# A fused spectral filter and MLP on one core: the sync queue in program order in the dense part as well

## The chip, the core and the metric

One NeuronCore of a Trainium2 chip. Its engines have queues of their own: PE (TensorE, matrix products into PSUM, with PEld loading the weights), ACT (ScalarE), DVE (VectorE), POOL (GpSimd) and SP (SyncE), which computes nothing here and issues DMAs. ACT and POOL issue some DMAs too. Each queue takes its instructions strictly in turn, so an instruction that waits on a semaphore holds up all behind it. The metric is the device time of one run in microseconds; lower is better.

## The reference, cut to what matters

```python
# x (8, 3008, 256) f32; filt_r, filt_i (1505, 256) f32
X = np.fft.rfft(x, axis=1)
Y = X * (filt_r + 1j * filt_i)[None]
x2 = np.fft.irfft(Y, n=3008, axis=1).astype(np.float32).reshape(24064, 256)
h = x2 @ w_in                       # w_in (256, 2048), float64
out = ((h - np.tanh(h)) @ w_out).astype(np.float32)   # w_out (2048, 256)
```

## The kernel before, in words

**Transforms.** 3008 is 64 x 47, so a transform is done as small matrix products in stages. `first` multiplies x by a 64-point matrix and writes `ct1` in DRAM; `middle` reads it back turned (tile `a2`, load_a2, L329), multiplies by a 47-point matrix (`pz`, L377), by the filter (`ft`, L335; the tiles `uv`, `zs`) and by the inverse matrix (`pe`, L358), and writes `ct2`; `last` reads that as `e2` (L409, L412), does the last product (`pu`) and leaves tokens in `ut` and combinations of them in `tu`. Matrices of middle come in as `fg` (load_slots, L322). The batches are taken as five units, `UNITS = [(0,), (1, 2), (3, 4), (5, 6), (7,)]`.

**Dense part.** The tokens form 48 groups of up to 512 (6 for a single batch, 12 for a pair). A group has four dense steps U (u = 0 to 3), each with 512 of the 2048 hidden columns: `up` (seven products of half-size blocks in place of eight), `shrink` for the step before (the activation, on ACT, DVE and POOL) and `down` for the one before that (accumulated in four PSUM banks over the four steps). Each dense step is cut into five quarters, at whose ends `t(k)`, k = 0 to 4, runs what is put between: a step of `first` or `middle` of the next unit, by the due times in `steps`, a stage of `late` (conversion of the last three eighths of the raw float64 weights, two raw tiles at a time) at even k, a stage of `copies` at odd k. A group is 20 quarters long. While unit 0's 24 dense steps run, first and middle of unit 1 are done among them, and so on.

**Stores.** When a group's accumulation is done, `down` leaves tile `o` in `stores`. At k = 2 of the next dense step `store` transposes it on DVE into `ot` (L624, one buffer) and issues 32 DMAs of 16 KB (12 KB in a unit's short last chunk) on the sync queue (L634).

**Copies.** `filters_d` zeroes some rows and then copies the filters from their input layout to `filt` in DRAM, for the units 1 to 4, one chunk of four frequencies in each of eight stages; `filters_of(c, filt_d)` issues at least six DMAs from DRAM to DRAM on the sync queue (L793). Unit 0 uses its own filters instead: `filters_of(c)` with no target loads a chunk into SBUF through POOL's queue (also L793), with a memset on POOL for the first three chunks, and `double_filters` copies it to the other half of the partitions on ACT (L818).

**Prologue.** Before the dense part, first (`first0`) and middle of unit 0 and the conversion of the first five eighths of the weights (raw loads, L195) run under `tc.manual_schedule()`: all queues in program order. Its last load is e2 of group 0. Then `last(0)` and the first two raw loads of `late` are traced with no order given.

**What sets the order.** The dense loop ran under `tc.manual_schedule(engines=order)` with PE, ACT, DVE and POOL: these take program order. SP is not among them; for it the framework's scheduler places each DMA by its own model as soon as its operands and buffers allow, so a DMA traced in the dense loop whose input is there from the start can stand among those of the prologue. Buffers are handed out by tag: a load into a tile waits until the tile that had the buffer has been read for the last time (`x` has three buffers, `a2`, `ft`, `fg`, `e2` two).

Of the kernel before, what the change touches and what calls it, by code (L numbers as in the profile page):

```python
# [140 lines left out]
def kernel(  # L141
# [9 lines left out]
    nc = tc.nc  # L151
    V, G, ACT = nc.vector, nc.gpsimd, nc.scalar
# [13 lines left out]
    def dram(t, off, dims):  # L166
        return bass.AP(tensor=t, offset=off, ap=[list(d) for d in dims])
# [100 lines left out]
    def halves(p, r, n):  # L268

        return [(h, slice(64 * h, 64 * h + 64), r + HALF * h, min(n, NR - r - HALF * h))  # L270
                for h in range(2) if r + HALF * h < NR]
# [144 lines left out]
    def widths(p, c):  # L416

        r, n = CHUNKS[p][c]
        return [128 if len(UNITS[p]) == 2 or r + j + HALF < NR else 64 for j in range(n)]
# [132 lines left out]
        gs[U] = (blocks, t, w)  # L552
        yield

    accs, stores = {}, []

    def down(U):

# [56 lines left out]
    def store(i, o):  # L615


        p, c = groups[i]
        r, n = CHUNKS[p][c]
        ws_ = widths(p, c)  # L620
        total = sum(ws_)
        ot = dn.tile([128, 2, CH * 128], F32, tag="ot", bufs=1, name="ot")
        for h in range(2):
            V.transpose(ot[:, h, 0:total], o[:, h, 0:total])  # L624
        b = UNITS[p][0]
        if len(UNITS[p]) == 2:
            blocks = [(r + 32 * q * NR, n, 32 * q) for q in range(4)]
        else:
            blocks = [(r_h + 32 * q * NR, n_h, rows.start + 32 * q)
                      for _, rows, r_h, n_h in halves(p, r, n) for q in range(2)]  # L630
        for h in range(2):
            for k in range(4):
                for row, m, lo in blocks:
                    nc.sync.dma_start(  # L634
                        dram(out.tensor, (b * SEQ + row) * DM + h * 128 + 32 * k,
                             [[NR * DM, 32], [DM, m], [1, 32]]),
                        ot[32 * k:32 * k + 32, h, :].rearrange(
                            "p (j c) -> p j c", c=128)[:, 0:m, lo:lo + 32])

    def bounded(z):  # L640

# [96 lines left out]
    with tc.tile_pool(name="tr", bufs=2) as tr:  # L738
        with tc.tile_pool(name="pro", bufs=1) as pro, \
# [83 lines left out]
            def turned(g3, t):  # L823


                ACT.copy(t[0:RP], g3[IM:IM + RP])
                ACT.mul(t[IM:IM + RP], g3[0:RP], -1.0)
# [11 lines left out]
            with tc.manual_schedule():  # L839
                nc.sync.dma_start(wf1, wf1_d)  # L840
                V.memset(near_b, B)
                V.memset(exp_b, -896.0)
                xs = [load_x0(0, (0, 4, 8))]
                ws = weights(tiles0, range(5), 3)
                xs += [load_x0(1), load_x0(2)]

                pad = pro.tile([64, DM], F32, name="pad")
                G.memset(pad, 0.0)
                G.dma_start(dram(ct1[0], NR * 64 * DM, [[DM, 64], [1, DM]]), pad)
                fts = {0: filters_of(0), 1: filters_of(1)}  # L850
                gx = [pro.tile([IM + RP, 4, RP2], F32, name=f"gx{k}") for k in range(2)]
                for t in gx:
                    G.memset(t[32:64], 0.0)
                next(ws)
                for c in range(3):
                    for k, _ in enumerate(first0(xs[c], c)):
                        if k == 3 or k == 1 and c > 0:
                            next(ws)
                G.dma_start(s2, s2_d)
                a2 = {0: load_a2(0, 0, False)}  # L860
                mats = {0: load_slots(0, pro), 1: load_slots(1, pro)}
                next(ws)
                double_filters(fts[0], 0)
                turned(mats[0][1], gx[0])
                waiting = []

                def back0():
                    j, uv, zs = waiting.pop(0)
                    c = j // 2
                    pe = z0("pe", [128, 2, DM])  # L870
                    for i in range(2):
                        k = (2 * j + i) % 4
                        nc.tensor.matmul(pe[0:RP2, i], mats[c][1][:, k], uv[0:IM + RP, i],
                                         start=True, stop=False)
                        nc.tensor.matmul(pe[0:RP2, i], gx[c % 2][:, k], zs[0:IM + RP, i],
                                         start=False, stop=True)
                    e1 = tr.tile([RP2, 2, DM], F32, tag="e1", bufs=2, name="e1")
                    ACT.copy(e1, pe[0:RP2])
                    ACT.dma_start(dram(ct2[0], 2 * j * RP2 * DM,
                                       [[DM, RP2], [2 * RP * DM, 2], [1, DM]]), e1)  # L880

                for j in range(NK // 2):
                    c = j // 2
                    if j % 2 == 0 and c + 1 < NK // 4:
                        a2[c + 1] = load_a2(0, c + 1, False)
                        if c + 2 < NK // 4:
                            mats[c + 2] = load_slots(c + 2, pro)
                            fts[c + 2] = filters_of(c + 2)
                    pz = z0("pz", [128, 2, DM])
                    for i in range(2):  # L890
                        k = (2 * j + i) % 4
                        nc.tensor.matmul(pz[:, i], mats[c][0][0:R2, k],
                                         a2[c][0:R2, k * DM:k * DM + DM], start=True, stop=True)
                    if waiting:
                        back0()
                    uv = tr.tile([128, 2, DM], F32, tag="uv", bufs=2, name="uv")
                    zs = tr.tile([128, 2, DM], F32, tag="zs", bufs=2, name="zs")
                    ft = fts[c][:, :, j % 2 * 2:j % 2 * 2 + 2]
                    V.tensor_mul(uv, pz, ft[:, 0])
                    V.tensor_mul(zs, pz, ft[:, 1])  # L900
                    waiting.append((j, uv, zs))
                    next(ws, None)
                    if j % 2 and c + 1 < NK // 4:
                        double_filters(fts[c + 1], c + 1)
                        turned(mats[c + 1][1], gx[(c + 1) % 2])
                    if j == NK // 2 - 2:
                        fs = first(1, z1)
                        next(fs)
                back0()
                for _ in ws:  # L910
                    pass
                e2s[0] = load_e2(*groups[0])


        with tc.tile_pool(name="dn", bufs=2) as dn, \
                tc.tile_pool(name="ps", bufs=1, space=bass.MemoryType.PSUM) as ps:

            psums.append(ps)
            for _ in last(0, z1):
                pass  # L920

            def tiles1(k, dtype, n):

# [21 lines left out]
                    yield  # L945

            late, copies = weights(tiles1, range(5, 8), 2), filters_d()
            next(late)
            total = 4 * len(groups)
            order = {nc.tensor.engine, ACT.engine, V.engine, G.engine}  # L950
            with tc.manual_schedule(engines=order):
                for U in range(total + 2):
                    i, u = divmod(U, 4)
                    if U < total:
                        p, c = groups[i]
                        if c == 0 and u == 0:
                            units = 4 * len(CHUNKS[p])
                            steps, done = [], 0
                            if p + 1 < len(UNITS):
# [3 lines left out]
                                lo, hi = 1.6 * units, 5 * units - 17  # L963
# [27 lines left out]
                    def t(k):  # L991


                        nonlocal ms, done
                        if k == 2 and stores:
                            store(*stores.pop())
                        if U >= total:
                            return
                        pos = 20 * c + 5 * u + k
                        if u == 3 and k in (0, 2) and i + 1 < len(groups):  # L1000
                            next(lasts)
                        elif done < len(steps) and steps[done] <= pos:
                            if done < n_f:
                                next(fs)
                            else:
                                next(ms)
                            done += 1
                            if done == n_f:
                                ms = middle(p + 1, z1)
                                next(ms)  # L1010
                        if i == len(groups) - 1 and k in (0, 2, 4):
                            next(bounds, None)
                        if k in (0, 2, 4):
                            next(late, None)
                        elif U > 0:
                            next(copies, None)
# [11 lines left out]
                            t(k)  # L1028
                for w in stores:
                    store(*w)  # L1030

    within = nc.values_load(count[0:1, 0:1], min_val=0, max_val=128)
    with tc.If(within < 128):
# [33 lines left out]
```

## Time and profile before

| | us |
|---|---|
| median of 7 runs | 2883.11 (2880.23 to 2887.02) |
| the profiled execution | 2884.76 |
| its span | 2883.0 |
| PE busy | 2749.3 |
| PE busy, from 300 to 2800 us | 2464.5 of 2500 |
| first dense product (`x`, L470) starts at | 130.2 |
| last store (32 DMAs) starts at | 2861.5 |

The page counts busy time by engine and cuts the span in 40 slices, one digit each, in tenths. Windows give the same for stretches that one names, with the share of time that the 16 DMA engines were busy. A row of waits reads "engine, line that waited <- what ended the wait: us in total, times, longest". SPq is SP's queue: a DMA's row there is the time SP took to issue it, not the transfer.

### The profile page before, as it was taken

The numbers are of one execution on the slowest core, as the hardware profiler recorded it, in microseconds if no ns is written. First come the engines' busy times: TensorE is split into PE (matmuls) and PEld (weight loads), VectorE is DVE, ScalarE is ACT, GpSimd is POOL, SyncE is SP. The second block draws the span as 40 slices with busy tenths as digits, with TensorE's granted clock in tenths as the row PEclk, the third lists the DMA queues.
The fourth block names the chain that finished last, engine by engine and source line by source line (L and its number), as shares of the span: only waits on it lengthen the run. The fifth ranks groups of instructions, "written<-read, shape, count | busy, mean of one in ns | idle before, by whom it ended". The sixth has DMA issues, their size and how long they took to land.

```text
span 2883.0 us, 36472 instructions
## 1 busy us (share of the span) xinstructions
PE 2749.3 (95%) x12474; PEld 2278.6 (79%) x12474; DVE 1983.3 (69%) x2214; ACT 1871.4 (65%) x2460; POOL 1747.7 (61%) x1379
## 2 busy tenths in 40 slices
PE   4789999999999999999999999999999999999996
PEld 2567677888878787888877887888888888888885
DVE  3585666766767777766676777766777777777765
ACT  3566666666667676666666776666666666666663
POOL 4345777445677767645576777655466666555544
PEclk7899999999999999999999999999999999999998
DMA  8763433232133222222222232312123222110100
GB/s 244 211 188 100 112 102 91 82 101 83 49 72 88 76 67 58 65 86 81 72 68 75 68 79 72 76 42 66 36 54 77 54 53 49 31 28 15 22 8 16
DMA packets 328030, 217.47 MB, mean 75 GB/s; under 512 B 229053, under 2 KB 280373, under 8 KB 327642
## 3 DMA queue, kind: packets, MB, share of 16 engines
q1 hardware_dynamic: 273464, 162.00, 22.9%
q10 hardware_dynamic: 52418, 49.82, 5.7%
q0 software_dynamic: 1952, 3.22, 0.5%
q8 instruction: 100, 1.64, 0.2%
q14 instruction: 96, 0.79, 0.1%
HBM read 138.81 MB, written 79.17 MB: 76 GB/s over the span
## 4 chain that ended last, share of the span: by engine, by line
PE 67%; ACT 10%; DVE 9%; POOL 4%; issue 4%; DMA 3%; SPq 1%; ACTq 1%; DVEq 0%; POOLq 0%
PE o L577 26%; PE x L470 17%; PE z L470 8%; PE y L470 5%; PE pe L358 3%; DVE h L531 3%; PE pu L434 3%; ACT y L526 2%; PE pz L377 2%; PE pf L298 2%; ACT y L527 2%; ACT u L476 1%; POOL t L452 1%; DVE h L535 1%; DVE uv L392 1%
## 5 line engine op out<-in xcount | busy, mean ns | idle before, releaser
L577 PE MATMUL o<-t,wd 128*128 128x256 f32 (+2 forms) x3072 | 779.0, 376 | 1.8 <-POOL t L451 1.3
L531 DVE TENSOR_TENSOR h<-h,y 128x1024 f32<-128x1024 f32 (+2 forms) x384 | 588.6, 1533 | 252.6 <-ACT y L527 252.5
L449 POOL TENSOR_TENSOR t<-h 128x512 f32<-128x512 f32 (+2 forms) x192 | 240.2, 1251 | 741.3 <-DVE h L535 561.2
L577 PEld LDWEIGHTS o<-t,wd 128*128 128x128 f32 x3072 | 582.1, 191 | 75.1 <-POOL t L451 1.9
L470 PE MATMUL x<-tu,wu 128*128 128x256 f32 (+2 forms) x2304 | 589.5, 378 | 14.0 <-ACT u L476 13.0
L577 PE MATMUL o<-h,wd 128*128 128x256 f32 (+2 forms) x2304 | 581.3, 375 | 0.2 <-DVE h L535 0.2
L535 DVE SCALAR_TENSOR_TENSOR h<-sq,h 128x1024 f32<-128x1024 f32 (+2 forms) x384 | 566.3, 1475 | 21.2 <-DVE h L531 0.9
L470 PEld LDWEIGHTS x<-tu,wu 128*128 128x128 f32 x2304 | 428.4, 190 | 156.5 <-issue 72.7
L577 PEld LDWEIGHTS o<-h,wd 128*128 128x128 f32 x2304 | 430.8, 190 | 71.1 <-issue 18.5
L532 ACT ACTIVATE sq<-y,near_b 128x1024 f32<-128x1024 f32 (+2 forms) x384 | 435.3, 1134 | 5.6 <-DVE h L535 0.9
L476 ACT COPY s<-x 128x512 f32<-128x512 f32 (+2 forms) x192 | 110.8, 577 | 461.7 <-PE x L470 450.7
L526 ACT ACTIVATE y<-h 128x1024 f32<-128x1024 f32 (+2 forms) x384 | 400.1, 1042 | 14.8 <-ACT e L361 7.2
L527 ACT ACTIVATE y<-y 128x1024 f32<-128x1024 f32 (+2 forms) x384 | 399.3, 1040 | 12.1
L452 POOL TENSOR_TENSOR t<-t,h 128x512 f32<-128x512 f32 (+2 forms) x192 | 308.7, 1608 | 0.0
L476 ACT COPY u<-x 128x512 f32<-128x512 f32 (+2 forms) x384 | 219.3, 571 | 80.4 <-PE x L470 33.1
L393 POOL TENSOR_TENSOR zs<-zs,ft 128x512 f32<-128x512 f32 x112 | 166.9, 1490 | 139.5 <-ACT zs L391 139.4
L450 POOL TENSOR_TENSOR t<-h,t 128x512 f32<-128x512 f32 (+2 forms) x192 | 241.5, 1258 | 15.1
L451 POOL TENSOR_TENSOR t<-h 128x512 f32<-128x512 f32 (+2 forms) x192 | 249.5, 1299 | 0.0
L394 POOL TENSOR_TENSOR uv<-uv,zs 128x512 f32<-128x512 f32 x112 | 211.7, 1890 | 16.0 <-DVE uv L392 7.8
L470 PE MATMUL x<-ut,wu 128*128 128x256 f32 (+2 forms) x768 | 200.4, 384 | 14.2 <-DVE h L506 13.0
L470 PE MATMUL z<-tu,wu 128*128 128x256 f32 (+2 forms) x768 | 193.9, 375 | 1.6 <-DVE h L512 1.6
L470 PE MATMUL z<-ut,wu 128*128 128x256 f32 (+2 forms) x768 | 195.0, 376 | 0.0
(112 smaller groups left out, 3237.5 us busy)
## 6 DMA issues: line engine op xcount, KB each, us to landing
a<-ct SPq DMA_DIRECT2D x64, 384.0 KB
ct<-e ACTq DMA_DIRECT2D x128, 192.0 KB
ft<-filt SPq DMA_DIRECT2D x96, 256.0 KB
out_dram<-ot SPq DMA_DIRECT2D x1408, 16.0 KB
ct<-a ACTq DMA_DIRECT2D x80, 256.0 KB
x_sb<-in_x_dram SPq DMA_DIRECT2D x69, 256.0 KB
e<-ct SPq DMA_DIRECT2D x33, 512.0 KB
fg<-fg SPq DMA_DIRECT2D x40, 392.0 KB
```

Of the source, the lines that this page charges most:

```text
L449: G.tensor_sub(t[0], b[0][1], b[0][0])
L450: G.tensor_sub(t[1], b[1][1], t[0])
L451: G.tensor_sub(t[2], b[1][1], b[0][1])
L452: G.tensor_sub(t[3], t[1], b[1][0])
L470: nc.tensor.matmul(bank[:, k], wu[:, q - 1, (2 * u + k) * 128:(2 * u + k + 1) * 128], rhs[q - 1], start=(first and k == 0), stop=True, ski ...
L476: ACT.copy(t, X)
L526: ACT.activation(y[k], ht[k], AF.Arctan, scale=S)
L527: ACT.activation(y[k], y[k], AF.Square)
L531: V.tensor_mul(ht[k], ht[k], y[k])
L532: ACT.activation(sq[k], y[k], AF.Square, bias=near_b, scale=A)
L535: V.scalar_tensor_tensor(out=ht[k], in0=sq[k], scalar=K, in1=ht[k], op0=ALU.add, op1=ALU.mult)
L577: nc.tensor.matmul(product(q), wd[:, q - 1, (2 * u + k) * 128: (2 * u + k + 1) * 128], rhs[q - 1][:, k], start=(u == 0 and k == 0 and q == ...
```

## The change

SP joins the engines in program order for the dense part, and `last(0)` and the first raw loads of `late` move inside that block. `store` no longer issues its 32 DMAs but appends them to a list; `store_some(4)`, called in every quarter right after it, issues four, so that a group's stores take eight quarters; what is left goes out at the end. In the prologue the second chunk of unit 0's filters, on POOL's queue, is loaded after the three rounds of `first0` and the load of `s2` instead of before them.

```diff
-    accs, stores = {}, []
+    accs, stores, outs = {}, [], []
...
         for h in range(2):
             for k in range(4):
                 for row, m, lo in blocks:
-                    nc.sync.dma_start(
+                    outs.append((
                         dram(out.tensor, (b * SEQ + row) * DM + h * 128 + 32 * k,
                              [[NR * DM, 32], [DM, m], [1, 32]]),
                         ot[32 * k:32 * k + 32, h, :].rearrange(
-                            "p (j c) -> p j c", c=128)[:, 0:m, lo:lo + 32])
+                            "p (j c) -> p j c", c=128)[:, 0:m, lo:lo + 32]))
+
+    def store_some(n):
+        for dst, src in outs[:n]:
+            nc.sync.dma_start(dst, src)
+        del outs[:n]
...
-                fts = {0: filters_of(0), 1: filters_of(1)}
+                fts = {0: filters_of(0)}
...
                 G.dma_start(s2, s2_d)
+                fts[1] = filters_of(1)
...
             psums.append(ps)
-            for _ in last(0, z1):
-                pass
...
             late, copies = weights(tiles1, range(5, 8), 2), filters_d()
-            next(late)
             total = 4 * len(groups)
-            order = {nc.tensor.engine, ACT.engine, V.engine, G.engine}
-            with tc.manual_schedule(engines=order):
+            with tc.manual_schedule():
+                for _ in last(0, z1):
+                    pass
+                next(late)
                 for U in range(total + 2):
...
                         if k == 2 and stores:
                             store(*stores.pop())
+                        store_some(4)
                         if U >= total:
                             return
...
                 for w in stores:
                     store(*w)
+                store_some(len(outs))
```

## The prediction

> **What bounds the kernel now.** I read the page first, for the engine that is busy and the slices in which it is not.
>
> ```profile
> span 2883.0 us, 36472 instructions
> PE 2749.3 (95%) x12474; PEld 2278.6 (79%) x12474; DVE 1983.3 (69%) x2214; ACT 1871.4 (65%) x2460; POOL 1747.7 (61%) x1379
> PE   4789999999999999999999999999999999999996
> DMA  8763433232133222222222232312123222110100
> ```
>
> PE is busy for 2749.3 of 2883.0 us, so all that an order of DMAs can win lies in 133.7 us of idle PE. The first slices (72 us each) hold most of it, and there DMA shows 8, 7, 6. The view by windows splits this up.
>
> ```profile
> core 0: us, PE busy (x) PEld busy (x) DVE busy (x) ACT busy (x) POOL busy (x), PEclk, DMA share, GB/s
> 20.00:40.00 20.00, 6.52 (x12) 2.14 (x10) 9.16 (x19) 6.70 (x13) 4.64 (x6) 0.66 0.96 304
> 40.00:60.00 20.00, 6.91 (x16) 5.06 (x17) 7.21 (x15) 5.51 (x8) 4.10 (x7) 0.50 0.81 223
> 60.00:80.00 20.00, 15.22 (x59) 10.27 (x58) 15.49 (x31) 14.46 (x21) 12.98 (x21) 0.93 0.93 254
> 80.00:100.00 20.00, 14.92 (x56) 10.49 (x56) 10.78 (x23) 9.91 (x15) 12.77 (x24) 0.89 0.99 241
> 300.00:2800.00 2500.00, 2464.52 (x11356) 2063.83 (x11354) 1764.41 (x1894) 1677.25 (x2183) 1579.47 (x1198) 1.00 0.26 64
> ```
>
> From 20 to 100 us the DMA engines are the limit (share 0.81 to 0.99, 255 GB/s in the mean) and PE works about half the time. From 300 to 2800 PE lacks only 35.5 us of 2500, with DMA at 0.26. Next, what SP put on its queue (start, time, line, DMA, count):
>
> ```profile
> 25.96 0.42 SPq L195 DMA_DIRECT2D raw<-in_moe_w_out_dram  x1
> 27.76 0.60 SPq L195 DMA_DIRECT2D raw<-in_moe_w_out_dram  x1
> 28.41 6.35 SPq L793 DMA_DIRECT2D filt<-in_filt_r_dram  x3
> 38.22 3.65 SPq L793 DMA_DIRECT2D filt<-in_filt_r_dram  x3
> 238.97 15.08 SPq L634 DMA_DIRECT2D out_dram<-ot  x32
> 254.09 0.91 SPq L329 DMA_DIRECT2D a<-ct  x2
> ```
>
> The first four lines are work of the dense part that SP takes in the middle of the prologue: the last raw weights, and filters copied from DRAM to DRAM. The last two are a group's 32 stores in one run, with the first load of the next unit's middle stage behind them. Last, who waited.
>
> ```profile
> PE pz L892 <- DMA fg<-fg: 13.7, 1, 13.7
> PE pz L377 <- DMA a<-ct: 2.1, 1, 2.1
> ACT a L773 <- DMA filt<-in_filt_i_dram: 3.4, 1, 3.4
> SPq L634 <- DVE ot L624: 681.3, 41, 41.2
> SPq L322 <- PE pe L358: 206.0, 19, 28.1
> ```
>
> PE's only long wait for a DMA is in the prologue. The second line is the load of 254.09. The third is ACT held up before a store of the prologue by a filter copy: the instruction records show SP's and ACT's DMAs taking turns on eight semaphores, each DMA waiting until the one before it on its semaphore has landed. The two SP rows are long, but SP waiting costs nothing unless a load behind it is late.
>
> **The change, step by step.**
>
> *Early DMAs leave the prologue.* With SP in program order, what the dense part traces cannot be issued before the prologue's last load (the e2 load, at 120.56). So the two raw loads at 25.96 and 27.76 go (2 x 512 KB, by the page's DMA list), and of the 39 L793 copies issued on SP before 125 us, the 19 that start before 97 us. Six copies move one chunk: 2 x (96 + 64 + 28) = 376 KB, so 19 are 1.19 MB. Together 2.24 MB; at 255 GB/s that is 8.8 us of a stage whose DMA engines are busy 0.92 of the time: 8.1 us. On the chain of waits from 24.8 to 99.9 us the DMA landings (7.73, 5.71, 5.25, 5.43, 8.90, 3.10, 11.76) are 47.9 of 75 us; if only they shrink, it is 8.8 x 0.64 = 5.6. Bounds: 3.4, the one wait that names such a copy, and 8.8. I take 7, nearer the bandwidth figure because the share is so near 1. The e2 load has 18 copies issued from 101.8 to 116.4 ahead of it and takes 4.31 us to land on the chain; without them 0 to 1.5 less, 0.5 taken. **-7.5.**
>
> *filters_of(1) on POOL's queue moves behind the s2 load.* A memset (1.82) and six DMAs (about 0.55 each), now from 7.1 to 17.7, come after POOL's wu subtractions at 35.2 and s2. Its 376 KB leave the first 20 us (202 GB/s: at most 1.9 us gained there) and come back in the next 30. On POOL, filters_of(2), issued from 38.9 to 44.1, moves 5.1 us back. Covers: chunk 1 is issued by about 45 and takes up to 9.8 us to land, for use by ACT at 61.4; chunk 2 would land near 59, for use at 67.9. If the prologue gets 7 us faster, both covers are nearly gone, so 0, with ends -1.9 and +3. **0.**
>
> *Work that was early is now in the fill of the dense part.* Job 0's three DVE instructions on its raw load ran at 115.7 to 119.8, when DVE was idle (0.93, 0.42, 0.43); they now follow last(0) in the fill: 0 to 1.8, +1 taken. The raws are issued behind e2's four DMAs (2.4 us), land some 5 us later, and are first used about 12 us after e2's issue; that cover is enough. **+1.**
>
> *39 copies now run beside the dense steps U = 2 to 5.* At 0.76 us they are 29.6 us of SP's time over about 72 us, and 2.4 MB or 9.6 us of DMA where the share is 0.53 (window 157:230). Queued behind them are x loads, traced 2.7 quarters (about 9 us) ahead of use, against 4.6 us for a batch of six; so they stay hidden. What may show is ACT waiting on a copy's semaphore before its ct stores: eight batches, from nothing to the 3.4 us of the prologue's row but mostly beside PE's work: 0 to +8, +1 taken as DMA is far from full here. **+1.**
>
> *Stores four to a quarter.* 32 x 0.47 us is a 15.1 us run on SP; the load at 254.09 now has at most four of them (1.9 us) ahead. PE's 2.1 us wait goes, and part of the following uv waits: the windows 250:300 and 300:350 lack 4.7 and 1.6 us of PE, so 3.0, ends 0 and 4.7. **-3.** Late next is the POOL product chain of uv, already PE's releaser there. The other 47 runs won't pay: after 300 us no PE wait names a DMA, although loads often stand behind 32 stores (0, end -3 for ACT's 5.5 us on out_dram). At the end the last 32 stores still go out in one run from 2861.48. **0.**
>
> The Trainium skill, "Trace Analysis", section DMA Optimizations, advises one DMA-capable engine for inputs and another for outputs; the change leaves both on SP. The same skill's page "DMA: Bandwidth & Descriptors", section Issuing engines are not separate DMA queues, calls the time to initiate a DMA usually small beside the DMA. Against the second stands the row above: 32 stores take SP 15.08 us. By that rule the term of -3 would be 0 and the sum 3 us higher; by the first, spreading is half a remedy, with 1.9 us left before each load.
>
> Sum: -7.5 + 0 + 1 + 1 - 3 = -8.5. The profiled execution took 2884.76 us (span 2883.0 and 1.8 around it), 1.65 above the median of the seven runs. 2884.76 - 8.5 - 1.65 = 2874.6; I say **2874.5 us**.
>
> **Rivals.**
>
> *Given back in the fill.* The prologue's 7.5 us come, but the dense steps 1 to 5, where DVE is 59 of 73 us busy (157 to 230) and PE still lacks 5.6 us, now carry the copies as well, and the ends above fall together (+1.8, +8, no gain at 254 beyond 2): about 2882. For it: ACT's waits have a price already; against it: DMA share 0.53 there.
>
> *Slower: SP blocked by its own order.* Middle's fg load waits for the other fg buffer, whose last reader is the following step's pe product (L322 row: 206 us in 19 waits). In program order the a2, ft and stores traced behind it now wait too. It decides where steps are shortest: during unit 0, 64 steps in about 64.6 quarters of 3.45 us, so an a2/ft load has four quarters, 13.8 us. fg wait 3.45, stores 1.9, POOL's release of ft up to 8.9 and landing 4 make 18.2; 4.4 us late on up to 16 loads would be 70, though the ends seldom meet; a third of them gives +23, and 2897. It decides once SP lags over about 10 us. Against it: later units have 2.29 quarters to a step, and there loads behind 32 stores don't stall PE now.
>
> *More than forecast.* The semaphore turns cost the prologue more than bandwidth (SP L793's 6.35 us for three DMAs), and it is 15 us shorter: 2862.
>
> **How the numbers follow.** A measurement of this kernel tells about 0.2% (5.8 us) from no change: below 2877.3 is faster, above 2888.9 slower. Chances: forecast 0.48 (its own range 2866 to 2881; about a fifth of it above 2877.3), given back 0.20, slower 0.23, more 0.09. Faster 0.39 + 0.02 + 0.09 = 0.50; slower 0.23 and the far end of given back, 0.02, make 0.25; same 0.25. The range 2862 to 2893 leaves out the lower end of "more" and over half of "slower".
>
> **What would show it.** Right: no L793 on SP before the e2 load; that load issued 6 to 9 us before 120.56; GB/s lower in 20 to 60; L634 in runs of four; the first a2 load no later than 4 us after its stores begin; no PE wait on a2. Wrong: PE pz L377 or DVE uv L392 waiting for DMA a or ft between 260 and 500 us, ACT waiting for filt copies from 150 to 230, or the prologue's end unmoved, which would mean that its own loads, not the added ones, fill the DMA engines.

## The result, and the profile after

Over 26 runs of the changed kernel the median is 2879.82 us (2875.93 to 2887.24), against 2882.0 us for the kernel before in the 63 runs beside them. The ratio is 0.9994 with a 95% interval of 0.9989 to 0.9999: about 1.7 us faster, which is within the 0.2% set as no change. Forecast were 8.5 us. The profiled execution took 2880.52 us; its span is 4.3 us shorter than that of before.

The page of the changed kernel (span, busy time by engine, two rows of the 40 slices):

```profile
span 2878.7 us, 36465 instructions
...
PE 2752.8 (96%) x12474; PEld 2279.1 (79%) x12474; DVE 1984.6 (69%) x2214; ACT 1872.1 (65%) x2460; POOL 1745.9 (61%) x1379
...
PE   5789999999999999999999999999999999999996
...
DMA  9654443232233222222323232122233222110100
```

The windows of the changed kernel, at the places shown of before and at 250 to 300:

```profile
core 0: us, PE busy (x) PEld busy (x) DVE busy (x) ACT busy (x) POOL busy (x), PEclk, DMA share, GB/s
20.00:40.00 20.00, 7.03 (x14) 2.44 (x12) 11.54 (x24) 9.80 (x17) 6.87 (x9) 0.67 0.93 314
40.00:60.00 20.00, 10.31 (x33) 7.87 (x34) 7.07 (x15) 5.13 (x9) 8.45 (x14) 0.59 0.93 208
60.00:80.00 20.00, 15.43 (x58) 9.89 (x57) 14.35 (x29) 13.41 (x21) 13.96 (x24) 0.91 0.98 245
80.00:100.00 20.00, 15.10 (x49) 9.48 (x50) 11.71 (x24) 10.27 (x16) 10.73 (x19) 0.83 0.90 221
...
250.00:300.00 50.00, 43.80 (x171) 32.61 (x170) 28.24 (x34) 30.14 (x42) 31.45 (x23) 0.93 0.46 114
300.00:2800.00 2500.00, 2469.55 (x11385) 2068.91 (x11384) 1766.35 (x1899) 1679.96 (x2191) 1577.95 (x1200) 1.00 0.26 65
```

The prologue is as full of DMA as before (0.90 to 0.98 from 20 to 100 us). From 250 to 300 PE did 171 matmuls where before did 179, at a granted clock of 0.93 instead of 0.97. From 300 to 2800 PE has 5.0 us more work done. So something was lost where the stores were to win, and something was won where the forecast had nothing.

SP's timeline of the changed kernel (start, time, line, DMA, count):

```profile
23.71 0.42 SPq L195 DMA_DIRECT2D raw<-in_moe_w_out_dram  x1
...
25.59 0.60 SPq L195 DMA_DIRECT2D raw<-in_moe_w_out_dram  x1
...
117.78 2.42 SPq L412 DMA_DIRECT2D e<-ct  x4
131.75 0.38 SPq L195 DMA_DIRECT2D raw<-in_moe_w_out_dram  x1
132.18 2.78 SPq L277 DMA_DIRECT2D x_sb<-in_x_dram  x3
...
237.92 1.79 SPq L642 DMA_DIRECT2D out_dram<-ot  x4
239.82 0.37 SPq L329 DMA_DIRECT2D a<-ct  x1
...
242.14 16.06 SPq L642 DMA_DIRECT2D out_dram<-ot  x28
258.24 0.43 SPq L329 DMA_DIRECT2D a<-ct  x1
```

The copies (now L798) are gone from the prologue, but both raw loads still stand at 23.71 and 25.59. The e2 load comes at 117.78, 2.8 us earlier. The first a2 load goes out at 239.82 behind four stores, the second behind 28 in one run. The waits of the changed kernel, in the form explained before:

```profile
PE pz L898 <- DMA fg<-fg: 14.5, 1, 14.5
...
PE pe L358 <- POOL uv L394: 4.2, 1, 4.2
...
SPq L322 <- PE pe L358: 308.6, 23, 32.5
...
PE pf L298 <- DMA x_sb<-in_x_dram: 1.6, 2, 1.1
```

PE's wait for a2 is gone. In its place stands a wait of 4.2 us for POOL, which before did not have.

**Where it went.** All kernels here issue the same 12474 matmuls in the same order, so the start of the k-th matmul can be compared. Its *lead* is its time in the profile of before less its time in the other profile; a gain counts as kept if the lead stays. The experiments e1 to e10 are described below; "change, again" is a second profile of the same changed kernel (e5b). This table is worked out from the records of one profile each; the times at the head are those of before, with the place of each: the first dense product, behind the fill of the dense part, ahead of the last x load of unit 1 and behind it, behind the first a2 load, and behind POOL's first uv. From 535.9 to 1813.7 the transforms of units 2 and 3 run.

```
lead in us at       130.2 156.7 235.0 255.2 265.5 272.3 535.9 1813.7
                    first after ahead after after after        units
                    dense fill  of x  x     a2    uv           2, 3
change                2.9   0.8   0.4   0.2   4.2  -2.3   0.1   5.65
change, again         5.4   2.7   2.45  0.0   4.05 -1.45 -0.7   4.9
e1 filters back      -2.0  -4.0  -4.9  -6.2  -2.2  -7.7  -5.3   0.3
e2 one burst          2.6   0.1   1.6  -2.5  -0.35 -1.5  -1.8  -8.8
e3 spread only       -1.6  -2.3  -0.9  -0.9   3.1  -3.35 -1.0  -0.8
e4 e2 first           4.0   1.4   2.8  -1.2   2.8  -2.7  -0.3   5.1
e5 POOL move only    -2.1  -2.0  -2.0  -2.0  -1.8  -1.8  -1.9  -1.8
e6 e4 + DVE           5.1   3.3   2.4   2.1   6.1   6.1   6.5  12.0
e7 e4 + x ahead       2.3   2.05  1.5   1.5   5.5  -1.1   1.45  7.1
e8 e4 + DVE + x       4.4   3.8   5.1   5.1   9.1   9.1   9.4  15.1
e9 before + DVE       0.9   1.5   1.5   1.5   1.45  1.5   1.4   1.55
e10 change + DVE      2.9   0.0   0.1  -2.2   1.8   1.8   2.2   7.9
```

Two things limit it. The prologue of e9 is that of before and shows 0.9 at the first dense product, that of e3, the same as well, -1.6: so much does one profile scatter there. And in the changed kernel 1.7 us of the step from -2.3 to 0.1 arise near 505 us, where eight matmuls ran at half speed in before; the second profile has no such step. After 1813.7 the lead stays until 2760 and then moves by -1.7 to +3.3 us with the granted clock of the last stretch (2780 to 2830: 0.93 before, 0.90 and 1.00 in the two profiles of the change), which I count for nothing.

### The profile page after: what moved, and what is told of

It is laid out like the page before. It is cut to its first block, busy times and chain, and to the rows that moved or that the text cites. A ratio compares the mean times of both kernels' runs of the same rounds, so it can differ in the third digit from the quotient of the medians.

```text
span 2878.7 us, 36465 instructions
## 1 busy us (share of the span) xinstructions
PE 2752.8 (96%) x12474; PEld 2279.1 (79%) x12474; DVE 1984.6 (69%) x2214; ACT 1872.1 (65%) x2460; POOL 1745.9 (61%) x1379
## 4 chain that ended last, share of the span: by engine, by line
PE 70%; DVE 9%; ACT 8%; POOL 5%; issue 4%; DMA 3%; ACTq 1%; SPq 1%; DVEq 0%; POOLq 0%
PE o L577 28%; PE x L470 18%; PE z L470 8%; PE y L470 5%; PE pe L358 3%; PE pu L434 3%; PE pz L377 3%; DVE h L531 3%; ACT y L526 2%; PE pf L298 2%; ACT y L527 1%; POOL t L452 1%; ACT u L476 1%; DVE h L535 1%; DVE h L506 1%
## 5 line engine op out<-in xcount | busy, mean ns | idle before, releaser
L531 DVE TENSOR_TENSOR h<-h,y 128x1024 f32<-128x1024 f32 (+2 forms) x384 | 589.5, 1535 | 253.0 <-ACT y L527 253.0
L535 DVE SCALAR_TENSOR_TENSOR h<-sq,h 128x1024 f32<-128x1024 f32 (+2 forms) x384 | 566.0, 1474 | 21.2 <-ACT y L526 0.9
L393 POOL TENSOR_TENSOR zs<-zs,ft 128x512 f32<-128x512 f32 x112 | 165.8, 1480 | 144.3 <-ACT zs L391 144.2
L450 POOL TENSOR_TENSOR t<-h,t 128x512 f32<-128x512 f32 (+2 forms) x192 | 241.4, 1257 | 15.1
L394 POOL TENSOR_TENSOR uv<-uv,zs 128x512 f32<-128x512 f32 x112 | 211.2, 1886 | 15.9 <-DVE uv L392 7.6
L486 DVE TENSOR_TENSOR h<-y,s 128x512 f32<-128x512 f32 (+2 forms) x192 | 130.3, 679 | 93.7 <-PE y L470 81.4
```

The costliest lines, as they stand in the source:

```text
L450: G.tensor_sub(t[1], b[1][1], t[0])
L531: V.tensor_mul(ht[k], ht[k], y[k])
L535: V.scalar_tensor_tensor(out=ht[k], in0=sq[k], scalar=K, in1=ht[k], op0=ALU.add, op1=ALU.mult)
```

## The experiments

Each ran beside the kernel before, in five rounds on one chip: e1 to e4 on one chip, the others on another. So ratios are to be compared, not times.

### The second filter chunk back at its place (e1)

```diff
-                fts = {0: filters_of(0)}
+                fts = {0: filters_of(0), 1: filters_of(1)}
...
                 G.dma_start(s2, s2_d)
-                fts[1] = filters_of(1)
```

> The changed kernel with the second chunk of unit 0's filters loaded where it was, ahead of the first products. Two theories of why the prologue's end (the issue of the e2 load) came only 2.8 us earlier (117.78 instead of 120.56) and not 7.5. Theory A, the two 512 KB raw loads of the dense part are still in the prologue and take its DMA time: then this edit changes little, e2 issued at 117 to 119 and the time within 2 us of the changed kernel. Theory B, the chunk moved back on POOL's queue holds up the prologue (ACT's copy at 75.80 waits for a filter load): then the e2 load is issued at 113 to 115.5 and the kernel is 2 to 4 us faster than the changed one.

2882.67 us, ratio 0.9993 (0.9984 to 1.0002). The e2 load was issued at 122.58, later than either theory had it, and PE's wait for fg was 16.5 us against 14.5. The first dense product came 4.9 us later than in the change. So in this profile taking the copies out of the prologue, the step priced at 7 us, gave nothing by itself; the move on POOL's queue, priced at 0, carries the gain together with it. From 40 to 60 us its DMA share was 0.73, where before had 0.81: room in the DMA engines that didn't make the prologue shorter. Its runs are as fast as the change's (0.9993 and 0.9994), so that they don't show the 5 us which its one profile keeps to 1813.7.

### That move alone (e5)

```diff
-                fts = {0: filters_of(0), 1: filters_of(1)}
+                fts = {0: filters_of(0)}
...
                 G.dma_start(s2, s2_d)
+                fts[1] = filters_of(1)
```

> The kernel before with one edit: the second chunk of unit 0's filters loaded after the first products and s2, as in the change. The run with the chunk back in its place had lost about 5 us by the first dense product against the changed kernel. If the move itself is what made the prologue shorter: first dense product 3 to 5 us earlier than before (at 125 to 127 instead of 130.2) with all copies and raws still in the prologue; the end 1 to 4 us earlier. If that loss was a difference of single executions: first dense product within 1.5 us of before, same time.

Made in the kernel before: 2883.13 us, ratio 1.0001 (0.9990 to 1.0012), e2 load at 122.69, first dense product 2.1 us later. Alone it is worth nothing either. With both, the lead at the first dense product is 2.3 to 5.4 us in eight profiles out of eight; with neither it is -1.6 to 0.9, and with one of them -2.0 and -2.1, one profile each. So the profiles say that the two gain only together, on thin evidence for either alone; why they don't add is not shown.

### The change again (e5b)

> The changed kernel once more, for a second profile. If the prologue's steps are the kernel's and not the execution's: e2 load issued at 117 to 118.5, the loss of about 6 us of lead between 265 and 275 us and the gains near 1105 and 1785 at the same places, within 0.5 us each. Otherwise the single profiles scatter by 2 us and more and carry less.

2878.01 us, ratio 0.9989 (0.9978 to 1.0001), with the e2 load at 115.09, 2.7 us earlier than in the first profile of the same program. It tells how much of a prologue's difference one profile can carry, and of the later steps it repeats those at a2 (4.0 us won), at uv (6.5 and 5.5 lost) and after 535.9 (5.5 and 5.6 won), but not those at the late x load (0.2 and 2.4 lost) and from uv to 535.9 (2.4 and 0.7 won).

### A group's stores in one burst, SP in program order (e2)

```diff
-                        store_some(4)
+                        store_some(len(outs))
```

> The changed kernel, but a group's 32 stores issued in one run again, with SP in program order. If the 1.7 us that PE gains near 1105 and near 1785 us come from ACT's ct store no longer finding a fresh store on its semaphore, these two go again and the first a2 load of unit 1's middle is issued 14 us later (near 254), PE waits for it again; time 2 to 6 us longer than the changed kernel. If program order alone gives them, the time stays within 1 us of the changed kernel.

2894.32 us, ratio 1.0033 (1.0022 to 1.0045): about 11 us slower than the change, more than either expectation had. A row of its waits, and a stretch of its SP timeline:

```profile
PE pf L298 <- DMA x_sb<-in_x_dram: 12.7, 6, 2.9
```

```profile
688.69 15.47 SPq L642 DMA_DIRECT2D out_dram<-ot  x32
704.25 1.54 SPq L277 DMA_DIRECT2D x_sb<-in_x_dram  x3
```

Three loads of x stand behind 32 stores, and PE waits for x for 12.7 us in all (1.6 in the profile of the change, 5.4 in its second). Four of the six waits, 7.7 us, lie after 580 us, and the lead falls by 12 us at these four. So the program order by itself is a loss, and the spreading pays back what the order costs. Two gains which I had thought to come from the spreading, 1.8 us each near 1105 and 1785 us, are here as well: they come from the order.

### The spreading without the order (e3)

```diff
-                    nc.sync.dma_start(
+                    outs.append((
...
+                        store_some(4)
...
+                store_some(len(outs))
```

> The kernel before with only the stores spread, four to a quarter, SP's order left to the scheduler and the prologue as it was. If the dense part's gains come from the spreading, it shows them from 300 us on (about 4 us by 1800) without the prologue's: 2 to 4 us faster than before. If program order is needed for them, 0 (within 1.5 us of before). The e2 load stays at 120 to 121 in both.

Made in the kernel before, with SP left to the scheduler: 2886.63 us, ratio 1.0004 (0.9995 to 1.0014). It wins 4.0 us at the first a2 load and loses 6.5 us seven us later, as the change does, and has no gain near 1105 or 1785.

**Where the order wins.** Between 535.9 and 1813.7 us the lead of all eight profiles with SP in program order and stores four at a time rises by 5.4 to 5.7 us (the change: 5.55 and 5.6); of the three without the order by 0.1 to 0.2. ACT's timeline of before shows what was there:

```profile
1100.34 0.57 ACT L361 COPY e<-pe 96x512 f32<-96x512 f32 x1
1103.37 0.32 ACTq L363 DMA_DIRECT2D ct<-e  x1
1103.79 0.58 ACT L476 COPY u<-x 128x512 f32<-128x512 f32 x1 [2.88 <-DVE h L535]
```

and that of the changed kernel at the same instructions:

```profile
1099.29 0.57 ACT L361 COPY e<-pe 96x512 f32<-96x512 f32 x1
1100.27 0.32 ACTq L363 DMA_DIRECT2D ct<-e  x1
1100.69 0.58 ACT L476 COPY u<-x 128x512 f32<-128x512 f32 x1 [0.83 <-DVE h L531]
```

In before the ct store goes out 2.46 us after its copy ends, and the next ACT copy, which PE needs, stands behind it; the bracket names DVE, but that was done. By the instruction records the store shares its completion semaphore with a store that SP had issued at 1101.76, and waits until that has landed: the last update of the semaphore comes at 1103.30, and ACT's wait on it ends at 1103.33. Counted from the end of the copy, or of the store before it on ACT, before has ten such delays of over 0.9 us after 260 us, 17.6 us in all; e3 nine (16.0), e5 nine (16.2), e9 eight (15.0); the change, e2 and e8 none. PE loses less than ACT, as most of them lie beside other work: 1.1 us near 808, 1.8 near 1104, 0.9 near 1490 and 1.75 near 1784, which is all of the 5.5. In e2 the same gains stand beside its greater losses. That the order takes the delays away is shown; how is not, since SP and ACT still share the eight semaphores in the changed kernel.

### The e2 load ahead of the raw loads (e4)

```diff
-                e2s[0] = load_e2(*groups[0])
...
             with tc.manual_schedule():
+                e2s[0] = load_e2(*groups[0])
                 for _ in last(0, z1):
                     pass
```

> The changed kernel with the e2 load of group 0 traced as the first DMA of the dense block, so that the two raw loads behind it cannot be issued in the prologue. Theory A: 1.05 MB less at 210 to 310 GB/s, e2 issued 3 to 4.5 us earlier, at 113.3 to 114.8, if the raws then land before their first use the kernel is 1 to 4 us faster than the changed one. Theory B: e2 load within 1 us of 117.8, and the raws landing late in the fill cost 0 to 2 us.

The block in program order for the prologue and the one for the dense part are two, and nothing puts the second behind the first: its first DMAs, which need nothing, still run ahead. With the e2 load as the dense block's first DMA, they queue behind its first half. 2878.47 us, ratio 0.9979 (0.9970 to 0.9988), about 4 us faster than the change's 0.9994 (0.9989 to 0.9999). SP's timeline:

```profile
116.72 1.14 SPq L412 DMA_DIRECT2D e<-ct  x2
117.90 1.10 SPq L195 DMA_DIRECT2D raw<-in_moe_w_out_dram  x2
119.05 1.12 SPq L412 DMA_DIRECT2D e<-ct  x2
```

The e2 load itself is only 1 us earlier than in the change, within the scatter, and the lead at 1813.7 is no larger than the change's (5.1 against 5.65 and 4.9). Against the change's second series (0.9989, 0.9978 to 1.0001) the intervals overlap. So the runs speak for a gain, but no profile shows where it arises.

### The first uv of a unit off POOL (e10, e9, e6)

PE's timeline of the changed kernel about the new wait, then POOL's:

```profile
259.73 1.89 PE L577 MATMUL o<-h,wd 128*128 128x256 f32 x8
265.79 2.02 PE L358 MATMUL pe<-uv,fg 112*96 112x512 f32 x2 [4.17 <-POOL uv L394]
267.60 1.91 PE L470 MATMUL x<-tu,wu 128*128 128x256 f32 x4
```

```profile
261.03 1.27 POOL L452 TENSOR_TENSOR t<-t,h 128x512 f32<-128x512 f32 x1
262.27 1.26 POOL L393 TENSOR_TENSOR zs<-zs,ft 128x512 f32<-128x512 f32 x1
263.60 2.13 POOL L394 TENSOR_TENSOR uv<-uv,zs 128x512 f32<-128x512 f32 x1
```

The same instructions of before, on PE and on POOL:

```profile
266.20 1.07 PE L358 MATMUL pe<-uv,fg 112*96 112x512 f32 x2 [0.36 <-DVE uv L392]
267.11 1.03 PE L470 MATMUL x<-tu,wu 128*128 128x256 f32 x4
```

```profile
262.45 1.27 POOL L393 TENSOR_TENSOR zs<-zs,ft 128x512 f32<-128x512 f32 x1
263.80 1.27 POOL L394 TENSOR_TENSOR uv<-uv,zs 128x512 f32<-128x512 f32 x1
```

PE stands for 4.17 us until POOL has made uv, and POOL comes to it only after four steps on the tile t. Before, the same pair of products on POOL started at 262.45, after the same four steps: there PE came late to `pe` by its wait for a2, and so never met POOL. Of the 4.2 us of lead 3.8 go in this wait. The matmuls after it take 2.02 and 1.91 us where before they took 1.07 and 1.03; with one more of 1.91 that is 2.7 us, and the lead is -2.3. The Trainium skill, "TensorE: Matmul & The Clock Gate", Part 1, says that TensorE falls to half its clock after an idle window of about 3.4 us; the rows agree: 4.17 us idle, and some 5 us at half speed after it. They don't agree everywhere: in e4 and e2 an idle time of 2.07 and 2.15 us was followed by slow matmuls too (see e7), and there the measurement decides.

```diff
-            G.tensor_mul(rows(zs), rows(zs), fi)
-            G.tensor_add(uv, uv, zs)
+            E = V if p == 1 and j == 0 else G
+            E.tensor_mul(rows(zs), rows(zs), fi)
+            E.tensor_add(uv, uv, zs)
```

> The changed kernel with the first middle step of unit 1 on DVE and nothing else. Theory: the lead at matmul 750 stays where it is at 725 (about +4 instead of -2), 5 to 6 us gained over the changed kernel there, ratio to before 0.997 to 0.998. Rival: the gain is taken back by 520 us, where the changed kernel won 1.7 us.

In the change: 2875.52 us, ratio 0.9973 (0.9963 to 0.9984), 6 us faster than the change, or 4.6 by the change's second series. PE's timeline has no such wait:

```profile
262.11 1.89 PE L578 MATMUL o<-h,wd 128*128 128x256 f32 x8
264.36 1.10 PE L358 MATMUL pe<-uv,fg 112*96 112x512 f32 x2 [0.35 <-DVE uv L392]
265.29 1.03 PE L471 MATMUL x<-tu,wu 128*128 128x256 f32 x4
```

> The kernel before with the first middle step of unit 1 on DVE and nothing else. Theory: there PE waits 2.1 us for the a2 load behind the 32 stores first, and what POOL delivers at 265.7 comes just in time after that, so without the stores out of the way the edit gives 0 to 1.5 us (lead at matmul 750 within 1.5 of 0): the two hold-ups stand one behind the other. Rival: POOL's load there costs on its own, then 3 to 5 us.

In the kernel before: 2880.15 us, ratio 0.9991 (0.9981 to 1.0002), and the lead through this stretch stays as it was (1.5, 1.45, 1.5), with PE's wait of 2.1 us for a2 still there. So two hold-ups stood one behind the other. Either edit alone leaves the other one, and only both together win the 4 us.

> The run with the e2 load first in the dense block, with one edit: the first step of unit 1's middle does its product zs and its sum uv on DVE instead of POOL. Theory: the 2.1 us wait for the a2 load only gave way to POOL, which is busy with the combinations t until 262.3 and delivers uv at 265.7 in both kernels; PE stands 4.2 us and then runs at a lower clock. It expects no wait of PE on POOL uv there, lead over the kernel before at matmul 750 of +2 to +4 us instead of -2.7, and 4 to 6 us off the time of that run (ratio to before 0.996). Rival: PE is held there by something else (the a2 or ft load), then the wait stays under another name and the time within 1.5 us.

On top of e4: 2874.13 us, ratio 0.9973 (0.9962 to 0.9985); the lead stays 6.1 through 272.3, where e4 falls from 2.8 to -2.7. The runs show less than the 4 to 6 us expected: 0.9973 against e4's 0.9979 is 1.7 us, within both intervals.

### x loaded three chunks ahead (e7)

```diff
-        xs = {c: load_x(p, *chunks[c]) for c in range(2)}
+        xs = {c: load_x(p, *chunks[c]) for c in range(3)}
...
-            if c + 2 < len(chunks):
-                xs[c + 2] = load_x(p, *chunks[c + 2])
...
+            if c + 3 < len(chunks):
+                xs[c + 3] = load_x(p, *chunks[c + 3])
             yield
```

> The run with the e2 load first in the dense block, with one edit: first loads x three chunks ahead, behind its product, instead of two. Theory: in program order the third x load stands behind a raw load that waits for DVE's conversion, so PE waits for x and 2 to 3 us of the prologue's gain go by 137 us. It expects the lead at matmul 258 to stay above +2.5 (it fell from 4.0 to 0.8), no PE wait on x_sb, and 1 to 3 us off that run's time. Rival: the lead is lost to ACT and DVE in the fill anyway: lead at matmul 300 within 1 us of 1.4, time the same.

On top of e4: 2875.77 us, ratio 0.9974 (0.9964 to 0.9984). From the first dense product to 156.7 the change loses 2.1 us and its second profile 2.7, e4 2.6; e7 loses 0.3. The reason is in SP's timeline above: the third x load, at 132.18, stands behind the raw load of 131.75, which waits until DVE has emptied its buffer. Traced ahead of it, x is there in time.

A second such place is the last x load of unit 1. SP's timeline of the change's second profile, and the row of PE's that answers to it:

```profile
222.56 5.88 SPq L798 DMA_DIRECT2D filt<-in_filt_r_dram  x5
228.49 3.92 SPq L798 DMA_DIRECT2D filt<-in_filt_i_dram  x5
232.51 0.35 SPq L277 DMA_DIRECT2D x_sb<-in_x_dram  x1
```

```profile
236.90 0.67 PE L298 MATMUL pf<-x_sb,wf_sb 128*128 128x256 f32 x2 [2.18 <-DMA x_sb<-in_x_dram]
```

The load stands behind ten copies, which take SP 9.9 us, and PE waits for it: 2.18 us here, 2.07 in e4, 2.15 in e2, 2.03 in e10. In e4 and e2 the eight matmuls next but one then run at about half speed (3.46 and 3.12 us against 1.89; in the change's second profile and in e10 they take 1.89), so that they lose 4.0 and 4.1. In the first profile of the change PE waited for almost nothing; in both its lead is 0.2 or less behind this place. What goes with the loss is the time that the ten copies take SP: 8.4 and 8.6 us in the first profile of the change and in e6, which lose 0.2 and 0.3 us here, and 9.5 to 9.9 us in the second, e1, e2, e4 and e10, which lose 1.3 to 4.1. Why the copies take longer in some profiles is open. e7 and e8 lose nothing here.

The whole-run gain over e4 (0.9974 against 0.9979) lies within both intervals.

### All three together (e8)

> The changed kernel with the three edits together: e2 load first in the dense block, first middle step of unit 1 on DVE, x three chunks ahead. If their gains add: ratio to before about 0.9965 (10 us off), lead at matmul 750 of +5 to +8 us. If x three ahead only moves the wait to the next DMA: ratio 0.997 to 0.998, as with the DVE edit.

The change with the edits of e4, e6 and e7: 2868.50 us, ratio 0.9951 (0.9936 to 0.9966), 14 us faster than the kernel before, where 10 were expected, and the fastest here. The page:

```profile
span 2864.3 us, 36451 instructions
...
PE 2740.1 (96%) x12474; PEld 2272.5 (79%) x12474; DVE 1988.1 (69%) x2216; ACT 1872.6 (65%) x2460; POOL 1744.3 (61%) x1377
```

Whether the parts add up depends on where the DVE step is read: 1.7 us of the change, 4.3 of e4 (0.9994 to 0.9979), 1.4 of the x loads (0.9979 to 0.9974) and 6.1 of the DVE step in the change (0.9994 to 0.9973) make 13.5, but with the 1.7 that the runs give it on top of e4 they make 9. By the lead at 1813.7, e8's 15.1 is 10 us above e4's 5.1; the DVE step alone adds 6.9 to e4 and the x loads 2.0.

## Why the prediction was right or wrong

The forecast of 2874.5 us missed the median by 5.3 us, and of its gain of 8.5 us 1.7 came. That the median still lies in the range given owes more to errors that cancel than to the steps: gains taken back and a gain not forecast.

**Early DMAs leave the prologue, -7.5.** Wrong in one half, too large in the other. The two raw loads, 1.05 of the 2.24 MB, did not leave: the step took program order in the dense block for order behind the prologue. The copies left, but e1 shows that bandwidth was the wrong price for them: without them, and without the POOL move, the prologue was no shorter. With the move the first dense product came 2.9 and 5.4 us earlier. The signs I had named say so as well: the windows 20 to 60 did not drop in both halves (304 to 314 GB/s, 223 to 208), and the e2 load came 2.8 and 5.5 us earlier, not 6 to 9.

**The POOL move, 0.** Wrong as part of the change: by e1, one profile, the change without it loses 4.9 us at the first dense product. Alone (e5) 0 was right for the time. I had weighed its two covers and not how it acts together with the copies.

**Work now in the fill, +1.** The size was 2.1 and 2.7, the mechanism another: not DVE's three instructions, but an x load behind a raw load on SP (e7). I had counted the raws' own landing, not what is queued behind them.

**Copies beside the dense steps, +1.** Small while they run, as far as two profiles tell: the lead falls by 0.4 and 0.25 us from 156.7 to 235.0, and no ACT wait between 150 and 235 names a copy. But behind the last ten stands an x load, and there 0.2 and 2.4 us more go. "About 9 us ahead of use" was the cover, and ten copies took SP 9.9 us: "so they stay hidden" failed by the landing. The ends, 0 and 8, hold it; its size goes with the time that the ten copies take (e7), not with how early PE arrives: e10 had a lead of 0.1 and lost 2.3, e6 had 2.4 and lost 0.3.

**Stores four to a quarter, -3.** The gain came, 4.0 us, by the mechanism named: the first a2 load 1.9 us after the stores begin, no wait for it in the dense part. It was then lost, with 2.5 and 1.5 us more. "Late next is the POOL product chain of uv" was the right name, put at nothing (though "already PE's releaser there" isn't in the rows of before: PE's waits at `pe` name DVE's uv, L392); that POOL's start does not depend on the a2 load (262.45 before, 262.27 after) could have been read from its order. Nor did "at most four" hold: with no load traced between them, 28 stores went out in one run of 16.06 us, since SP waits for nothing between quarters.

**The other 47 runs, 0.** Wrong by 5.5 us of gain, and by a mechanism I had seen in the prologue: ACT's stores and SP's DMAs sharing semaphores. Here I gave it only an end of -3, for the 5.5 us in which ACT's waits name SP's stores, and put it at 0 as no PE wait names a DMA. Of the ACT waits behind the ten delays two carry that name; others, behind the two largest gains among them, carry DVE's.

By the leads of the two profiles, then: prologue and move -2.9 and -5.4, all but 0.2 of it taken back in the fill and behind the copies (+2.7 and +5.4); +2.5 and +1.5 at the stores; -5.5 after. That is -3.2 and -4.0, without the 2.4 and 0.7 us won between 272.3 and 535.9, which in the first profile are for the most part slow matmuls of before. The spans moved by -4.3 and -8.5 and the runs by 1.7 and, in the second comparison, 3.2 us; what lies between I leave to the scatter of single profiles.

**Rivals.** *Given back in the fill* (2882) is what happened to the prologue's gain, by loads of x on SP rather than by DVE or ACT, and its time is 2.2 us from the median, though its own ends add up to 2883.4. It had nothing of the loss at POOL and of the gain after 800 us, which are larger, so that it came near is in part luck. *SP blocked by its own order* did not come: the L322 waits rose from 206.0 to 308.6 us, longest 32.5, well over its point of 10 us, yet no PE wait after 260 us names a, ft or fg. Its kin is real, though: e2 is 11 us slower than the change, by loads of x. The skill's rule of "DMA: Bandwidth & Descriptors", Issuing engines are not separate DMA queues, that the time to initiate a DMA is usually small, would have e2 equal to the change: here 32 stores took SP 15.47 us and decided it. Whether loads and stores on engines of their own would do better, no run here shows. *More than forecast* did not come for the change, and 15 us in place of 7.5 in the sum would be 2867, not 2862; e8 reaches 2868.5 by other edits.

## What to carry to other kernels

When a wait is taken away, look up when the next releaser of the same instruction is ready, from the order on its own engine: if that doesn't move, the gain ends there, and here a PE idle for 4.17 us cost 2.7 us more at a lower clock. A queue put in program order can rid another queue of waits (here ACT, 5.5 us) and loses by the loads that now stand behind stores and copies, so put the loads further ahead in the same step. And two blocks in program order are not in order with each other: a DMA that needs nothing goes first in whichever block it stands.

## What the runs showed of the hardware

- A store on ACT's queue can wait for a DMA that SP has just issued, if both signal on one semaphore: 1.0 to 2.5 us each, ten times in before, and of the ACT waits behind them only two name that DMA.
- After PE had stood for 4.17 us its matmuls took 2.02 and 1.91 us instead of 1.07 and 1.03, for some 5 us; after 2.03 to 2.18 us idle, matmuls soon after were slow in two profiles of four.
- The POOL add at 263.60 took 2.13 us, where the same add took 1.27 in before. It ran beside DVE's L531 and L535, and that L535 took 2.10 us in place of 1.23; in before DVE was idle during the add. In before as a whole, of the 97 operations of POOL's L393 and L394 that took over 1.9 us 86 ran beside DVE's L535 for over 0.3 us, of the 117 under 1.4 us four did.
- Two profiles of one program differ by 2.7 us in the issue of the e2 load, so a step of the prologue smaller than that needs more than one profile.
